# Head groups of 6, 7, 7, 6, 6, a second path for four token tiles, and another order of the first two units in a fused local-attention and gated-MLP kernel

## The chip, the core and the metric

The kernel runs on one core of a Trainium2 chip. The time of a run is in device microseconds (us), and lower is better. The engines are TensorE (PE, with its weight load PEld), VectorE (DVE), ScalarE (ACT), GpSimd (POOL) and SyncE (SP). DMA is issued from the queues of SP, ACT and POOL. Each engine runs its own instructions in the order in which they stand, and waits on semaphores for the others.

## What is computed

```python
xn = layernorm(x)                          # x: 2048 tokens of 640 features, f32
q, k, v = split(xn @ wqkv)                 # 32 heads of 20
# token t attends to t, t-2, ..., t-14 (window 8, dilation 2), masked below 0
s = softmax(q.k * 20**-0.5) @ v, then @ wo
g = silu(((xn @ w_gate) * (xn @ w_up)) @ w_down)   # hidden width 1536
out = x + s * g
```

All inputs are f32. Products are made at f32 accuracy by splitting each operand into a high part (fp32r) and a low part and adding three products: high by high, high by low, low by high.

## The kernel before

**Tokens.** Partition p holds 16 consecutive tokens, so a tile of 128 tokens takes one of the 16 from each partition. Tiles 0 to 7 are the even ones, 8 to 15 the odd ones, and so the neighbours at distance 2 stand in the same partition, in the next tile. Attention is then elementwise work on DVE over whole tiles. Only the first seven places come from the partition above, by a DMA that shifts k and v by one partition.

**Units and pieces.** A unit is one group of heads with one parity: `GROUPS` gives the heads of each of five groups, `UN` the ten units (u = 2 times group plus parity). `qkv(u, i)` makes q, k and v of one unit for one tile: 15 matmuls (three products by five feature blocks), with 3 x 20 x heads columns, into one of four `q` buffers of PSUM. ACT copies k and v into `kv` and q into one of two q tiles in SBUF. `attention(u)` is a generator of DVE work on the unit's tiles. `advance(budget)` draws some of its instructions into the program beside the matmuls, so that the order on DVE is written by these budgets. A piece is `gate_up(f, ch)`: 128 hidden columns by 512 tokens (four tiles), 15 matmuls for gate and 15 for up. `finish` multiplies the two: on DVE where an attention is running, else on ACT and POOL. Each unit after the second is followed by some pieces. Then follow the output projection and a down projection of 112 products.

**From x to the transposed operand.** Every matmul needs xn with features on partitions, split into high and low (`xT_tile`; four tiles share an `xc` buffer). There are two ways:

- Tiles 0 to 7: DVE takes the moments (`moments`), works out 1/std (`rstd`) and normalizes in place (`apply`). PE transposes five blocks of 128 columns into PSUM (`trans`, line 243), ACT copies the high part (line 244), DVE subtracts for the low part (line 245).
- Tiles 8 to 15: the moments are taken from the tile as it is first loaded. Then the tile is loaded again over itself from `xq` (`load_xq`), a copy in HBM in which the quarters of the tokens and of the features have changed places, so that VectorE's transposes within blocks of 32 finish the job (`trans_odd`). A row there holds quarters of four tokens, so the means and 1/std are spread to the right rows by small matmuls against a selection matrix (`spread`, line 263), and each tile is normalized in four pieces of 160 columns. ACT copies the high part, DVE subtracts the low part (line 275).

**The start.** PE first multiplies the identity with itself (`idle_product`) until operands are there. Weights are loaded raw (`wraw`, three buffers, in the order of the SP queue) and split: high part on ACT (line 85), low part on POOL (line 86), in later groups by a DMA that adds. Before, the program goes: tiles 0 and 1, their qkv of unit 0, half of the first piece, tiles 2 and 3, and so on, with tiles 8 to 15 prepared while PE does unit 0 and the pieces of the first two hidden blocks; then all eight tiles of unit 1; the attention of unit 0 is started during unit 1.

Of the kernel before, what the change touches and what calls it, by code (L numbers as in the profile page):

```python
# [13 lines left out]
AF = mybir.ActivationFunctionType  # L14
# [5 lines left out]
P = 128  # L20
S, D, F = 2048, 640, 1536
H, DH = 32, 20
W, DIL = 8, 2
# [27 lines left out]
def kernel(  # L51
# [114 lines left out]
    ident = st([P, P], "lg", 2)  # L166
    make_identity(nc, ident)

    def idle_product():

        nc.tensor.matmul(pt([P, 3, P], "q", 4), ident, ident.unsqueeze(1).to_broadcast([P, 3, P]), start=True,
                         stop=True)

    for _ in range(4):
        idle_product()
    eps_t = st([P, 1], "eps", 1)
    nc.vector.memset(eps_t, EPS)

# [15 lines left out]
    def moments(s0, n, mv=None):  # L194
        stats = st([P, n, 2, 6], "stats", 2)
        mv = st([P, n, 2], "mv", 2) if mv is None else mv
        for i in range(n):
            for a in range(2):
                nc.vector.bn_stats(stats[:, i, a, :], xt[s0 + i][:, a * HALF:(a + 1) * HALF])
            nc.vector.bn_aggr(mv[:, i, :], stats[:, i])  # L200
        return mv
# [20 lines left out]
    def apply(y, m, r):  # L222
        nc.vector.tensor_scalar(y, y, m, r, op0=ALU.subtract, op1=ALU.mult)
# [14 lines left out]
    def trans(s, later=False):  # L238
        hi, lo = xT_tile(s)
        for k0, k1 in ((0, 4), (4, KD)):  # L240
            p = pt([P, k1 - k0, P], "q", 4)
            for k in range(k0, k1):
                nc.tensor.transpose(p[:, k - k0, :], xt[s][:, k * P:(k + 1) * P], ident)  # L243
            nc.scalar.activation(hi[:, k0:k1, :], p, AF.Copy)
            halves.append(lambda p=p, k0=k0, k1=k1: nc.vector.tensor_sub(lo[:, k0:k1, :], p,  # L245
                                                                         hi[:, k0:k1, :].bitcast(F32)))
        if not later:
            low_parts()

    mvo = st([P, NE, 2], "mvo", 1)
    mro = st([P, 2, NE], "mro", 1)
    mrq = st([P, NQ, 2, NE], "mrq", 1)

    def load_xq(s, n, t):
        nc.sync.dma_start(t, xq[:, s - NE:s - NE + n, :])

    def spread():

        p = pt([P, NQ, 2, NE], "q", 4)
        for a in range(NQ):
            nc.tensor.matmul(p[:, a], sel[:, a], mro, start=True, stop=True)  # L263
        nc.scalar.activation(mrq, p, AF.Copy)

    def trans_odd(s):
        for a in range(NQ):
# [5 lines left out]
        nc.scalar.activation(hi, y, AF.Copy)  # L273
        low_parts()
        halves.append(lambda: nc.vector.tensor_sub(lo, y, hi.bitcast(F32)))
# [30 lines left out]
    def qkv(u, i, runs=ALL_RUNS, at=None, act=None):  # L306

        g, r = UN[u]
        c = GROUPS[g] * DH
        p = pt([P, 3 * c], "q", 4)  # L310
        t0 = (i % TPC) * P
        for n, (a, b, k) in enumerate(runs):
            if n == at:
                act()
            nc.tensor.matmul(p, xT[(r * NE + i) // TPC][a][:, k, t0:t0 + P], wq[g][b][:, k], start=n == 0,  # L315
                             stop=n == len(runs) - 1, skip_group_check=act is not None)
        nc.scalar.activation(kv_t[u][:, :, W - 1 + i, :], p[:, c:].rearrange("p (a c) -> p a c", a=2), AF.Copy)  # L317
        nc.scalar.activation(q_t[u][:, i, :], p[:, :c], AF.Copy)
# [91 lines left out]
    def gate_up_half(f, ch, n, p, c=slice(0, CH), **parts):  # L410
        mm3(p[:, c], [([t[:, k, n, :] for t in wf[f]], [t[:, k, c] for t in xT[ch]]) for k in range(KD)], **parts)
# [38 lines left out]
        while unfinished:  # L450
            unfinished.pop(0)()

    def gate_up_first(f, ch):

        pp = [pt([P, CH], "g", 2), pt([P, CH], "u", 2)]
        for parts, first in ((ALL3[:2], True), (ALL3[2:], False)):
            for n in range(2):
                gate_up_half(f, ch, n, pp[n], slice(0, CH // 2), parts=parts, first=first, last=not first)
        return pp


# [197 lines left out]
        return lambda: None  # L659


    norm(0, 1)
    mv1 = moments(1, 1)
    split_wq(0, nc.gpsimd, (0, 2))
# [2 lines left out]
    norm(1, 1, mv1)  # L667
    split_wq(0, nc.gpsimd, (3, KD))
    load_x(12, 1, xa[:, 0:1])
    begin_unit(0, False)  # L670
# [3 lines left out]
    qkv(0, 0, hh[:3] + lh[:3] + hh[3:] + lh[3:] + hl, 2 * KD + 3, lambda: trans(1))  # L674
    moments(3, 1, mv2[:, 1:2])
    load_x(13, 1, xa[:, 1:2])
    split_wf(0, nc.gpsimd, range(KD + 1))
    norm(2, 2, mv2)
    qkv(0, 1)
    split_wf(1, nc.gpsimd, range(KD + 1))  # L680
    zero_front(0)
    part0 = gate_up_first(0, 0)
    trans(2)
    trans(3)
    mask = st([1, NE, W], "mask", 1)
    nc.gpsimd.memset(mask, 0.0)
    for i in range(NE - 1):
        nc.gpsimd.memset(mask[:, i, :W - 1 - i], MASKED)
    sel = st([P, NQ, P], "ot", 2)
    nc.gpsimd.tensor_copy(sel.rearrange("p q (b i) -> p q b i", i=QB),  # L690
                          ident.rearrange("p (q i) -> p q i", i=QB).unsqueeze(2).to_broadcast([P, NQ, NQ, QB]))
# [8 lines left out]
    moments(10, 2, mvo[:, 2:4])  # L700
    load_xq(8, 4, xc[:, 4:8])
    trans(7)
    load_wf(2)
    qkv(0, 4)
    qkv(0, 5)
    moments(12, 2, mvo[:, 4:6])
    moments(14, 2, mvo[:, 6:8])
    load_xq(12, 3, xa)
    load_xq(15, 1, xd)
    nc.vector.tensor_copy(mro[:, 0, :], mvo[:, :, 0])  # L710
    rstd(mvo[:, :, 1], mro[:, 1, :], NE)
    gate_up(0, 1, amid=(spread,))
    trans_odd(8)
    trans_odd(9)
    qkv(0, 6)
    trans_odd(10)
    qkv(0, 7)
    trans_odd(11)
    gate_up(1, 1, amid=(lambda: trans_odd(12),))
    trans_odd(13)  # L720
    begin_unit(1)
    for i in range(8):
        if i == 3:
            running.append((0, attention(0)))
        if i == 2:
            load_wq(1, ((0, 3), (3, 5)))
            low_parts()
        if i < 2:
            trans_odd(14 + i)
        qkv(1, i)  # L730
        advance(PACE * 1.9)
    running.append((1, attention(1)))
    split_wq(1, nc.gpsimd)
    gate_up(0, 2)
    gate_up(1, 2)
    gate_up(0, 3)
    split_wf(2, nc.gpsimd)
    gate_up(1, 3)

    pieces = [(f, ch) for f in range(2, KF - 2) for ch in range(NCH)]  # L740
# [153 lines left out]
```

## Time and profile before

| | |
|---|---|
| time, median of 3 runs | 773.0 us (772.5 to 773.0) |
| time of the profiled execution | 772.99 us |
| its span, first to last instruction | 771.0 us |
| PE busy in the span | 763.1 us |
| DVE, ACT, POOL busy | 622.4, 251.2, 103.0 us |
| granted TensorE clock | 1.000 |

The profile page gives busy times, the chain of work that ended last, the costliest groups of instructions and the DMA issues. The span is 2.0 us shorter than the profiled execution's own time, and that time agrees with the median. A row of a timeline reads: start, length, engine, line, operation, what it writes and reads, count, and in brackets the idle time before it with what ended it. A row of the chain reads: start, length, engine, line. Lines are those of the kernel before; in the changed kernel the same code stands some lines lower.

### The profile page before, as it was taken

The page shows a single profiled execution, that of the slowest core. Times are in us where ns is not written, and L with a number is a line of the kernel's source. Part 1 is how long each engine was busy: PE and PEld are TensorE (multiplying, and loading weights), DVE is VectorE, ACT ScalarE, POOL GpSimd, SP SyncE. Part 2 cuts the span into 40 slices and gives each one's busy share as a digit, 9 for nine tenths or more (in the row PEclk, how much of TensorE's full clock was granted, in tenths as well). Part 3 has the DMA queues.
Part 4 walks back from the last instruction along what each step waited for, and adds up shares of the span by engine and source line. Part 5 has one row for each costly group of instructions (what it writes and reads, how often), then busy time and mean ns, then how long its engine had stood idle before and what let it go on. Part 6 is the DMA issues. An engine that isn't in the chain of part 4 may idle for free.

```text
span 771.0 us, 10626 instructions
## 1 busy us (share of the span) xinstructions
PE 763.1 (99%) x4214; PEld 703.7 (91%) x4214; DVE 622.4 (81%) x615; ACT 251.2 (33%) x519; POOL 103.0 (13%) x111
## 2 busy tenths in 40 slices
PE   8999999999999999999999999999999999999997
PEld 6889898898988989989899898888999999999997
DVE  6889899989959999599996999980377577777775
ACT  5333322132221241122411222213365564444442
POOL 5301110102001010000100000005387500000000
PEclk9999999999999999999999999999999999999999
DMA  9172441448043390423824213462887465555533
GB/s 323 73 235 83 90 119 55 87 148 144 28 112 75 100 203 29 115 62 113 176 55 115 63 57 101 107 179 66 201 248 217 168 250 175 193 185 185 184 103 137
DMA packets 82277, 103.33 MB, mean 134 GB/s; under 512 B 19036, under 2 KB 61376, under 8 KB 82100
## 3 DMA queue, kind: packets, MB, share of 16 engines
q1 hardware_dynamic: 72400, 82.85, 34.4%
q0 software_dynamic: 4128, 10.70, 8.1%
q10 hardware_dynamic: 5700, 9.11, 4.3%
q8 instruction: 33, 0.54, 0.3%
q14 instruction: 16, 0.13, 0.0%
HBM read 65.23 MB, written 28.31 MB: 121 GB/s over the span
## 4 chain that ended last, share of the span: by engine, by line
PE 97%; DMA 2%; ACT 0%; POOL 0%; DVE 0%; issue 0%; SPq 0%; POOLq 0%
PE q L315 26%; PE u L101 21%; PE g L101 21%; PE q L632 11%; PE q L101 9%; PE u L632 5%; PE g L632 3%; DMA wraw<-in_wgu 1%; DMA wraw<-in_wqkv 1%; PE q L243 0%; POOL wql L86 0%; ACT wf L85 0%; SPq L148 0%; PE q L263 0%; DVE xc L245 0%
## 5 line engine op out<-in xcount | busy, mean ns | idle before, releaser
L101 PE MATMUL u<-xc,wf 128*128 128x512 f32 (+1 forms) x735 | 171.8, 385 | 0.0
L101 PE MATMUL g<-xc,wf 128*128 128x512 f32 (+1 forms) x735 | 171.7, 385 | 0.0
L101 PEld LDWEIGHTS u<-xc,wf 128*128 128x128 f32 x735 | 136.0, 188 | 27.4
L101 PEld LDWEIGHTS g<-xc,wf 128*128 128x128 f32 x735 | 135.9, 188 | 26.6
L315 PE MATMUL q<-wqh,xc 128*128 128x420 f32 (+2 forms) x800 | 153.0, 334 | 2.0 <-DVE xc L245 1.2
L315 PEld LDWEIGHTS q<-wqh,xc 128*128 128x128 f32 x800 | 138.9, 188 | 3.8 <-DVE xc L245 1.4
L351 DVE TENSOR_TENSOR t<-q,kv 128x2240 f32<-128x2240 f32 (+2 forms) x40 | 90.6, 2286 | 28.8 <-DMA kv<-kv 28.6
L376 DVE TENSOR_TENSOR t<-lg,kv 128x2240 f32<-128x2240 f32 (+2 forms) x40 | 90.8, 2289 | 0.9
L355 DVE TENSOR_REDUCE lg<-t 128x112 f32<-128x2240 f32 (+2 forms) x40 | 90.5, 2281 | 0.0
L423 ACT ACTIVATE gs<-g 128x512 f32<-128x512 f32 x48 | 28.6, 596 | 174.0 <-PE g L101 164.9
L315 PE MATMUL q<-wql,xc 128*128 128x420 f32 (+2 forms) x400 | 81.8, 334 | 0.0
L317 ACT ACTIVATE kv<-q 128x280 f32<-128x280 f32 (+2 forms) x80 | 30.7, 383 | 139.4 <-PE q L315 137.4
L315 PEld LDWEIGHTS q<-wql,xc 128*128 128x128 f32 x400 | 69.9, 188 | 0.0
L384 DVE TENSOR_TENSOR t<-t,t 128x2240 f32<-128x2240 f32 (+2 forms) x30 | 68.7, 2289 | 0.8
L632 PE MATMUL q<-xc,wf 128*128 128x320 f32 x432 | 67.2, 309 | 0.0
L632 PEld LDWEIGHTS q<-xc,wf 128*128 128x128 f32 x432 | 64.3, 188 | 0.0
L92 POOL DMA_DIRECT2D wf<-in_wgu x10 | 8.7, 873 | 277.7 <-ACT wf L91 224.4
L101 PE MATMUL q<-wf,wf 128*128 128x320 f32 x156 | 35.5, 309 | 0.0
L92 POOL DMA_DIRECT2D wql<-in_wqkv x8 | 10.2, 1281 | 133.1 <-ACT wql L91 132.5
L101 PEld LDWEIGHTS q<-wf,wf 128*128 128x128 f32 x156 | 26.1, 188 | 0.0
L434 DVE TENSOR_TENSOR hs<-u,gs 128x512 f32<-128x512 f32 x38 | 25.9, 683 | 0.0
L86 DVE TENSOR_TENSOR wf<-ot,wf 128x640 fp32r<-128x640 f32 x13 | 14.2, 1091 | 12.8 <-ACT wf L85 12.8
(167 smaller groups left out, 919.4 us busy)
## 6 DMA issues: line engine op xcount, KB each, us to landing
h_scr<-hs SPq DMA_DIRECT2D x48, 256.0 KB, 2.2
wraw<-in_wgu SPq DMA_DIRECT2D x12, 640.0 KB, 6.6
wf<-in_wgu POOLq DMA_DIRECT2D x10, 640.0 KB, 6.3
t<-h_scr SPq DMA_DIRECT2D x8, 768.0 KB, 7.7
hs<-s_scr SPq DMA_DIRECT2D x16, 320.0 KB, 4.5
gs<-in_x SPq DMA_DIRECT2D x16, 320.0 KB, 4.9
wraw<-h_scr SPq DMA_DIRECT2D x12, 384.0 KB, 6.0
out<-q SPq DMA_DIRECT2D x14, 320.0 KB, 3.8
```

Of the source, the lines that this page charges most:

```text
L86: eng.tensor_sub(lo, raw, hi.bitcast(F32))
L92: nc.gpsimd.dma_start(lo, src, accum_op=ALU.add)
L101: nc.tensor.matmul(acc, a, b, start=first and n == 0, stop=last and n == len(runs) - 1)
L315: nc.tensor.matmul(p, xT[(r * NE + i) // TPC][a][:, k, t0:t0 + P], wq[g][b][:, k], start=n == 0, stop=n == len(runs) - 1, skip_group_check ...
L317: nc.scalar.activation(kv_t[u][:, :, W - 1 + i, :], p[:, c:].rearrange("p (a c) -> p a c", a=2), AF.Copy)
L351: nc.vector.tensor_mul(prods[j], q.rearrange("p i c -> p (i c)").unsqueeze(1).to_broadcast([P, 2, NE * c]), places(0, j))
L355: nc.vector.tensor_reduce(out=lg[:, :, j:j + 2].rearrange("p n a -> p a n"), in_=heads(prods.pop(j)), op=ALU.add, axis=AX.X)
L376: nc.vector.tensor_mul(heads(t), pw, heads(places(1, j)))
L384: nc.vector.tensor_add(acc, acc, t)
L423: nc.scalar.activation(gs, pp[0], AF.Copy)
L434: nc.vector.tensor_mul(hs, pp[1], gs)
L632: nc.tensor.matmul(p, y[:, i, k], wd_t[name][k][:, l], start=new and r == 0, stop=r == len(runs) - 1, skip_group_check=True)
```

## The change

1. `GROUPS` goes from 5, 6, 7, 7, 7 to 6, 7, 7, 6, 6 heads.
2. Tiles 4 to 7 take the second way too: loaded again from `xq` (which now holds tiles 4 to 15), normalized in quarters, transposed by VectorE. `spread` becomes one matmul for four tiles instead of four matmuls for eight: VectorE first puts each mean and 1/std into its own quarter (`mrb`).
3. Tiles 4 to 15 are done in three batches of four: moments, second load, `spread`, `trans_quarters`. Units 0 and 1 and the first two hidden blocks are interleaved in the same batches. The attention of unit 0 is started after the last batch.
4. The first eight pieces and unit 1 are followed by 2 pieces ahead of unit 2, and units 2, 3, 4 by 3, 3, 4 pieces (before: none, then 4 after each).
5. At the start: tiles 2 and 3 are normalized one at a time; tile 2 is transposed between the two halves of `gate_up_first` and tile 3 inside `qkv(0, 2)`; the zeros of kv, the mask and the selection matrix are made on POOL first of all; the last idle product has 256 columns instead of 384.

PE in the start, before (`q` is PSUM, `xc` the transposed operand, `t_67` tiles 2 and 3, `wf` gate and up weights, `lg_89` the identity):

```order
L101 MATMUL u_267<-xc_140,wf_209 128x256 x10
L101 MATMUL g_266<-xc_140,wf_210 128x256 x5
L101 MATMUL u_267<-xc_140,wf_210 128x256 x5
L243 MATMUL q_298<-lg_89,t_67 128x128 x4
L243 MATMUL q_304<-lg_89,t_67 128x128
L243 MATMUL q_309<-lg_89,t_67 128x128 x4
L243 MATMUL q_315<-lg_89,t_67 128x128
L315 MATMUL q_358<-wqh_134,xc_140 128x300 x5
L315 MATMUL q_358<-wql_135,xc_140 128x300 x5
```

The same place now:

```order
L102 MATMUL u_290<-xc_162,wf_238 128x256 x10
L244 MATMUL q_311<-lg_89,t_67 128x128 x4
L244 MATMUL q_317<-lg_89,t_67 128x128
L102 MATMUL g_289<-xc_162,wf_239 128x256 x5
L102 MATMUL u_290<-xc_162,wf_239 128x256 x5
L327 MATMUL q_332<-wqh_156,xc_162 128x360 x5
L244 MATMUL q_338<-lg_89,t_67 128x128 x4
L244 MATMUL q_344<-lg_89,t_67 128x128
L327 MATMUL q_332<-wql_157,xc_162 128x360 x5
```

Tile 2's transposes stand ten matmuls earlier, tile 3's five matmuls later than the first matmul of `qkv(0, 2)`.

DVE after the moments of tiles 4 to 7, before (`xc_81` holds these tiles as loaded):

```order
L219 TENSOR_SCALAR rstd_346<-rstd_346 128x4
L220 TENSOR_TENSOR r_345<-rstd_346 128x4
L223 TENSOR_SCALAR xc_81<-xc_81,mv_332,r_345 128x640 x4
L245 TENSOR_TENSOR xc_430<-q_431,xc_430 128x4x128
L245 TENSOR_TENSOR xc_430<-q_437,xc_430 128x128
L245 TENSOR_TENSOR xc_430<-q_442,xc_430 128x4x128
L245 TENSOR_TENSOR xc_430<-q_448,xc_430 128x128
```

and now:

```order
L221 TENSOR_TENSOR mro_108<-rstd_375 128x4
L264 TENSOR_TENSOR mrb_109<-mro_108,t_67 128x32
L224 TENSOR_SCALAR xc_81<-xc_81,mrq_110 128x160 x4
L282 STREAM_TRANSPOSE ot_446<-xc_81 128x640
L224 TENSOR_SCALAR xc_81<-xc_81,mrq_110 128x160 x4
L282 STREAM_TRANSPOSE ot_454<-xc_81 128x640
L287 TENSOR_TENSOR xc_448<-ot_446,xc_448 128x5x128
L224 TENSOR_SCALAR xc_81<-xc_81,mrq_110 128x160 x4
L282 STREAM_TRANSPOSE ot_500<-xc_81 128x640
L287 TENSOR_TENSOR xc_448<-ot_454,xc_448 128x5x128
```

Between the moments and the first normalizing instruction there are now the multiplication into quarters (L264), a matmul and a second load of 1280 KB (on their own engines); the transposes have gone from PE to DVE, and the low parts come between the tiles.

PE from the first full piece's up product to unit 0's second four tiles, before:

```order
L101 MATMUL u_461<-xc_140,wf_253 128x512 x10
L101 MATMUL u_461<-xc_140,wf_254 128x512 x5
L243 MATMUL q_517<-lg_89,xc_81 128x128 x4
L243 MATMUL q_523<-lg_89,xc_81 128x128
L315 MATMUL q_530<-wqh_134,xc_430 128x300 x5
L315 MATMUL q_530<-wql_135,xc_430 128x300 x5
L315 MATMUL q_530<-wqh_134,xc_430 128x300 x5
L315 MATMUL q_550<-wqh_134,xc_430 128x300 x5
L315 MATMUL q_550<-wql_135,xc_430 128x300 x5
L315 MATMUL q_550<-wqh_134,xc_430 128x300 x5
L101 MATMUL g_593<-xc_430,wf_209 128x512 x10
L101 MATMUL g_593<-xc_430,wf_210 128x512 x5
```

and now, from the spread on:

```order
L274 MATMUL q_439<-mrb_109,t_67 128x32
L102 MATMUL g_458<-xc_162,wf_277 128x512 x10
L102 MATMUL g_458<-xc_162,wf_278 128x512 x5
L102 MATMUL u_459<-xc_162,wf_277 128x512 x10
L102 MATMUL u_459<-xc_162,wf_278 128x512 x5
L327 MATMUL q_513<-wqh_156,xc_448 128x360 x5
L327 MATMUL q_513<-wql_157,xc_448 128x360 x5
L327 MATMUL q_513<-wqh_156,xc_448 128x360 x5
L327 MATMUL q_533<-wqh_156,xc_448 128x360 x5
L327 MATMUL q_533<-wql_157,xc_448 128x360 x5
L327 MATMUL q_533<-wqh_156,xc_448 128x360 x5
```

The transposes of tiles 6 and 7 are gone, and only one piece stands between the spread of the means and the four tiles' qkv, which now follow each other.

```diff
-GROUPS = [5, 6, 7, 7, 7]
+GROUPS = [6, 7, 7, 6, 6]
+FIRST = 4
...
-    for _ in range(4):
-        idle_product()
+    for n in (3, 3, 3, 2):
+        idle_product(n)
...
+    def moments_of_four(s):
+        a, b = s - FIRST, (s - FIRST) // 4
+        moments(s, 4, mvo[:, a:a + 4])
+        nc.vector.tensor_copy(mro[:, b, 0], mvo[:, a:a + 4, 0])
+        rstd(mvo[:, a:a + 4, 1], mro[:, b, 1], 4)
+        nc.vector.tensor_mul(mrb[:, b], mro[:, b].unsqueeze(1).to_broadcast([P, NQ, 2, 4]),
+                             blk.unsqueeze(2).unsqueeze(3).to_broadcast([P, NQ, 2, 4]))
...
+    def spread(s):
+
+        b = (s - FIRST) // 4
+        p = pt([P, NQ, 2, 4], "q", 4)
+        nc.tensor.matmul(p, sel, mrb[:, b], start=True, stop=True)
+        nc.scalar.activation(mrq[:, :, b], p, AF.Copy)
+
+    def trans_quarters(s):
+        b, i = divmod(s - FIRST, 4)
         for a in range(NQ):
-            apply(xt[s][:, a * QC:(a + 1) * QC], mrq[:, a, 0, s - NE:s - NE + 1], mrq[:, a, 1, s - NE:s - NE + 1])
+            apply(xt[s][:, a * QC:(a + 1) * QC], mrq[:, a, b, 0, i:i + 1], mrq[:, a, b, 1, i:i + 1])
...
+    begin_unit(0)
+    mask = st([1, NE, W], "mask", 1)
...
-    part0 = gate_up_first(0, 0)
-    trans(2)
-    trans(3)
...
-    norm(4, 4)
-    qkv(0, 2)
+    part0 = gate_up_first(0, 0, lambda: trans(2))
+    qkv(0, 2, at=KD, act=lambda: trans(3))
+    moments_of_four(4)
+    load_xq(4, 4, xc[:, 0:4])
     qkv(0, 3)
     gate_up(0, 0, part=part0)
-    trans(4)
-    trans(5)
-    moments(8, 2, mvo[:, 0:2])
-    gate_up(1, 0, amid=(lambda: trans(6),))
...
+    spread(4)
+    trans_quarters(4)
+    trans_quarters(5)
+    gate_up(1, 0)
+    trans_quarters(6)
+    trans_quarters(7)
+    low_parts()
+    for i in range(4, 8):
+        qkv(0, i)
+    load_wf(2)
+    moments_of_four(8)
     load_xq(8, 4, xc[:, 4:8])
...
+    gate_up(0, 1, amid=(lambda: spread(8),))
+    for i in range(8, 12):
+        trans_quarters(i)
+    low_parts()
+    moments_of_four(12)
...
+    gate_up(1, 1)
     begin_unit(1)
...
+    for i in range(4):
+        qkv(1, i)
+    gate_up(0, 2, amid=(lambda: spread(12),))
+    for i in range(12, 16):
+        trans_quarters(i)
+    low_parts()
+    running.append((0, attention(0)))
+    gate_up(1, 2)
+    for i in range(4, 8):
+        if i == 6:
+            gate_up(0, 3)
             load_wq(1, ((0, 3), (3, 5)))
-            low_parts()
...
+            split_wf(2, nc.gpsimd)
         qkv(1, i)
         advance(PACE * 1.9)
     running.append((1, attention(1)))
     split_wq(1, nc.gpsimd)
...
     gate_up(1, 3)
...
-    for u in range(2, len(UN)):
-        unit(u)
-        for _ in range(4 if u + 1 < len(UN) else len(pieces)):
+    COUNT = (0, 2, 3, 3, 4, 4, 4, 4, 4)
+    for u in range(1, len(UN)):
+        if u > 1:
+            unit(u)
+        for _ in range(COUNT[u] if u + 1 < len(UN) else len(pieces)):
```

More of the change, by code (lines that the diff above doesn't have):

```diff
@@ L167, with idle_product @@
     make_identity(nc, ident)
-    def idle_product():
-        nc.tensor.matmul(pt([P, 3, P], "q", 4), ident, ident.unsqueeze(1).to_broadcast([P, 3, P]), start=True,
+    def idle_product(n):
+        nc.tensor.matmul(pt([P, n, P], "q", 4), ident, ident.unsqueeze(1).to_broadcast([P, n, P]), start=True,
                          stop=True)
-    for _ in range(4):
-        idle_product()
+    for n in (3, 3, 3, 2):
+        idle_product(n)
     eps_t = st([P, 1], "eps", 1)
@@ L248, in trans @@
             low_parts()
-    mvo = st([P, NE, 2], "mvo", 1)
-    mro = st([P, 2, NE], "mro", 1)
-    mrq = st([P, NQ, 2, NE], "mrq", 1)
-    def load_xq(s, n, t):
-        nc.sync.dma_start(t, xq[:, s - NE:s - NE + n, :])
-    def spread():
-        p = pt([P, NQ, 2, NE], "q", 4)
-        for a in range(NQ):
[L263 to L267, printed above, removed]
-            apply(xt[s][:, a * QC:(a + 1) * QC], mrq[:, a, 0, s - NE:s - NE + 1], mrq[:, a, 1, s - NE:s - NE + 1])
+    NS = NT - FIRST
+    mvo = st([P, NS, 2], "mvo", 1)
+    mro = st([P, NS // 4, 2, 4], "mro", 1)
+    mrb = st([P, NS // 4, NQ, 2, 4], "mrb", 1)
+    mrq = st([P, NQ, NS // 4, 2, 4], "mrq", 1)
+    def moments_of_four(s):
[5 more added lines that the diff above has]
+                             blk.unsqueeze(2).unsqueeze(3).to_broadcast([P, NQ, 2, 4]))
+    def load_xq(s, n, t):
+        nc.sync.dma_start(t, xq[:, s - FIRST:s - FIRST + n, :])
+    def spread(s):
[5 more added lines that the diff above has]
+        b, i = divmod(s - FIRST, 4)
+        for a in range(NQ):
+            apply(xt[s][:, a * QC:(a + 1) * QC], mrq[:, a, b, 0, i:i + 1], mrq[:, a, b, 1, i:i + 1])
         y = st([P, KD, P], "ot", 2)
@@ L458, in gate_up_first @@
                 gate_up_half(f, ch, n, pp[n], slice(0, CH // 2), parts=parts, first=first, last=not first)
+            if first:
+                amid()
         return pp
@@ L659, in gather @@
         return lambda: None
+    begin_unit(0)
+    mask = st([1, NE, W], "mask", 1)
+    nc.gpsimd.memset(mask, 0.0)
+    for i in range(NE - 1):
+        nc.gpsimd.memset(mask[:, i, :W - 1 - i], MASKED)
+    sel, blk = xe[:, 2, :P], xe[:, 2, P:P + NQ]
+    nc.gpsimd.memset(blk, 0.0)
+    for a in range(NQ):
+        c = slice(a * QB, (a + 1) * QB)
+        nc.gpsimd.memset(blk[c, a:a + 1], 1.0)
+        nc.gpsimd.tensor_copy(sel[c].rearrange("p (q i) -> p q i", i=QB),
+                              ident[c, c].unsqueeze(1).to_broadcast([QB, NQ, QB]))
     norm(0, 1)
@@ L708 @@
+    load_wf(2)
+    moments_of_four(8)
+    load_xq(8, 4, xc[:, 4:8])
+    gate_up(0, 1, amid=(lambda: spread(8),))
[3 more added lines that the diff above has]
+    moments_of_four(12)
     load_xq(12, 3, xa)
     load_xq(15, 1, xd)
[L710 to L719, printed above, removed]
@@ L733 @@
     split_wq(1, nc.gpsimd)
[L734 to L737, printed above, removed]
     gate_up(1, 3)
@@ L872 @@
     arrays["xb"] = lay(arrays["x"].reshape(S, NQ, KD, QB).transpose(0, 2, 1, 3).reshape(S, D))
-    odd = arrays["x"].reshape(NQ, QB, NE, DIL, NQ, QC)[:, :, :, 1]
-    arrays["xq"] = lay(odd.transpose(3, 1, 2, 0, 4).reshape(P, NE, D))
+    tiles = arrays["x"].reshape(NQ, QB, NE, DIL, NQ, QC).transpose(4, 1, 3, 2, 0, 5).reshape(P, NT, D)
+    arrays["xq"] = lay(tiles[:, FIRST:])
     q3 = np.asarray(A_wqkv).reshape(D, 3, D)
```

30 lines of the change are left out of this document (4 added, 26 removed).

## The prediction

> **What bounds the kernel now.** I read the page's busy times first, then the chain that ended last, PE's waits and the windows.
>
> ```profile
> span 771.0 us, 10626 instructions
> PE 763.1 (99%) x4214; PEld 703.7 (91%) x4214; DVE 622.4 (81%) x615; ACT 251.2 (33%) x519; POOL 103.0 (13%) x111
> PE q L171 <- POOL lg masks.py:199: 1.4, 1, 1.4
> PE q L315 <- DVE xc L245: 1.2, 1, 1.2
> PE q L315 <- ACT xc L244: 0.9, 2, 0.6
> POOL wql L86 <- ACT wqh L85: 5.4, 1, 5.4
> 700.00:771.00 71.00, 66.59 (x455) 66.33 (x453) 51.31 (x69) 28.04 (x48) 0.00 (x0) 1.00 0.48 165
> ```
>
> PE is busy for 763.1 of 771.0 us. Its idle time is 1.4 + 1.2 + 0.9 at the start (the rows of waits give total, times, longest) and 4.4 in the last 71 us (66.59 busy), behind its last matmul. Between 20 us and the tail it never waits. So only two things move the end: the matmul time itself, and waits that are made or taken away. The chain shows the start and the pieces that the change touches (start, length, what):
>
> ```profile
> 9.31 7.81 DMA wraw<-in_wgu
> 17.14 1.65 ACT wf L85 x5
> 18.79 0.49 ACT xc L244
> 19.30 0.70 DVE xc L245
> 20.05 4.40 PE q L315 x30
> 24.44 1.79 PE g L101 x15
> 28.04 1.09 PE q L243 x10
> 32.55 0.55 PE q L243 x5
> 36.55 0.55 PE q L243 x5
> 44.68 0.80 PE q L263 x8
> 59.96 16.40 PE q L315 x120
> 76.36 3.40 PE g L101 x15
> 103.56 19.20 PE q L315 x120
> 196.36 22.40 PE q L315 x120
> ```
>
> The second gate/up block (issued 9.31, landed 17.12) is split on ACT ahead of the copies of tile 2; PE stands still until 20.05, and from there it is full.
>
> **PE's own work.** The unit rows (120 matmuls) give 16.40, 19.20 and 22.40 us for 5, 6 and 7 heads. Two units per group: before 2 x (16.40 + 19.20 + 3 x 22.40) = 205.6, after 2 x (3 x 19.20 + 2 x 22.40) = 204.8: **-0.8**. The transposes of tiles 4 to 7 go: 1.09 + 0.55 + 0.55 = **-2.2**. The spread took 0.80 for four matmuls; three remain at about 0.2 (twice the columns, so 0.2 to 0.4): **-0.2**, or +0.4 at worst. PE sum: -3.2. DVE, ACT and DMA rows that replace these lie beside PE unless they come late, which is the rest of this text.
>
> **The start.** Two of the sixteen tile products of unit 0 and 1 get wider ahead of the wait at 20.05: 2 x (19.20 - 16.40) / 8 = 0.7 us, which falls into that wait. So behind the wait PE loses not 0.8 but 1.5 us: **-0.7** more. Tile 3's transposes move from ahead of the wait to behind it: **+0.55**. The wait itself: PE used to need the low part on DVE, because its PSUM buffer was that of tile 2's first transposes. Now tile 3 comes later, the buffers turn differently, and PE needs only the first copy of ACT: -0.7 (the DVE row). Against that the weights grow.
>
> ```profile
> wraw<-in_wqkv SPq DMA_DIRECT2D x5, 150.0 KB, 4.0
> 7.00:11.00 4.00, 3.30 (x22) 2.52 (x20) 3.08 (x11) 2.06 (x7) 3.90 (x5) 1.00 0.98 346
> 11.00:15.00 4.00, 3.73 (x28) 3.51 (x27) 3.38 (x14) 3.43 (x12) 2.40 (x5) 1.00 1.03 403
> ```
>
> Five loads of 150 KB become 180: 0.154 MB more ahead of the awaited block, at 346 to 403 GB/s (last column) 0.4 us, since DMA is full (share 0.98 and 1.03). The block's issue also waits for POOL's splits, a fifth longer, but the queue is not empty by then. I take 17.12 + 0.45, PE full again at 17.57 + 1.65 + 0.02 + 0.49 + 0.07 = 19.8: **-0.25** (bounds -0.7 with no delay, +0.4 if issue sets it). The POOL work moved ahead of the first split lies in the 5.4 us that POOL waits before it (the last of the rows of waits), and the shorter idle product gains nothing behind that wait. Start: -0.7 + 0.55 - 0.25 = -0.4.
>
> **The new chain of tiles 4 to 7.** This is where a wait can arise. From 19.8 PE does a tile's qkv (2.4), tile 3's transposes (0.55), another qkv (2.4), half a piece (3.6), the spread (0.2), a piece (6.8): `qkv(0, 4)` starts at 35.8. Each tile's product needs the high part at once and the low part after ten of 15 matmuls, so tile 6's low part is wanted at 35.8 + 4.8 + 1.6 = 42.2. DVE's side:
>
> ```profile
> 20.90 0.88 DVE L199 BATCH_NORM_STATS2 stats<-xc 128x6 f32<-128x320 f32 x2
> 23.92 0.83 DVE L199 BATCH_NORM_STATS2 stats<-xc 128x6 f32<-128x320 f32 x2
> 26.24 0.16 DVE L220 TENSOR_TENSOR r<-rstd 128x4 f32<-128x4 f32 x1
> xc<-in_xq SPq DMA_DIRECT2D x1, 1280.0 KB, 6.7
> wraw<-in_wgu SPq DMA_DIRECT2D x1, 640.0 KB, 4.0
> 45.88 1.18 DVE L223 TENSOR_SCALAR xc<-xc,mrq 128x160 f32<-128x160 f32 x4 [1.89 <-DMA xc<-in_xq]
> 49.80 1.29 POOL L437 TENSOR_TENSOR hs<-hs,gs 128x512 f32<-128x512 f32 x1 [11.24 <-ACT hs L436]
> 50.33 1.45 DVE L275 TENSOR_TENSOR xc<-ot,xc 128x640 fp32r<-128x640 f32 x1 [0.33 <-ACT xc L273]
> 56.35 0.78 DVE L275 TENSOR_TENSOR xc<-ot,xc 128x640 fp32r<-128x640 f32 x1
> ```
>
> Tile 3's low part ends about 22.5 (19.8 + 0.8 of PE + 0.55 + 0.5 on ACT + 0.9 on DVE). The moments of four tiles take about 4.0 (20.90 to 23.92 plus one tile), so the second load is issued at 26.5: SP waits there, and behind it stand only writes of h and loads for later. The same 1280 KB took 6.7 us beside other loads; 640 KB alone took 4.0 (an answer for 109 to 118 us). Alone, 1280 KB should take 4.0 plus 655 KB at 403 GB/s = 5.6, an estimate from these rows. So it lands at 32.1 to 33.2. From the first normalizing piece to the third tile's low part the same code took 56.35 + 0.78 - 45.88 = 11.2 us, with 0.67 in it from one subtraction that took 1.45 instead of 0.78 while POOL multiplied. Tile 6 is ready at 43.3 to 44.4: 1.1 to 2.2 late; with the POOL product elsewhere and a load that lands by 31.4 it is in time. Bounds 0 and 2.2, and I take **+1.2** (near the lower row, since little else is loaded then). The Trainium skill (SBUF — State Buffer, Who interferes with whom) says that a VectorE instruction with two SBUF inputs and a GpSimd instruction that reads SBUF block each other; the 1.45 beside 0.78 agrees, and by that rule the product of the new piece near 36 us costs the same 0.67, which the 11.2 holds already.
>
> The spread itself waits on DVE's means: moments at 26.5 plus 1.6 for 1/std and the quarters (24.9 to 26.4 on DVE before, and one small multiplication), so 28.1 against PE's 28.8: no wait, 0.3 at worst. Only this spread has half a piece ahead of it; for the next batch the two sides meet almost evenly: DVE needs 0.8 + 4.0 + 1.7 = 6.5 behind tile 6's low part, PE has 0.8 + 2.4 + 3.4 = 6.6 to do. **+0.1** (0 to 0.5). Later batches: the load of tiles 8 to 11 is issued about 48 and has until 55, that of 12 to 15 about 69 with two pieces ahead: no wait at 5.6 to 6.7, with 1 to 3 us to spare.
>
> **Attention starts later.**
>
> ```profile
> 69.51 3.56 DVE L351 TENSOR_TENSOR t<-q,kv 128x1600 f32<-128x1600 f32 x2
> 138.55 4.22 DVE L351 TENSOR_TENSOR t<-q,kv 128x1920 f32<-128x1920 f32 x2
> 177.47 1.16 DVE L387 TENSOR_TENSOR q<-t 128x960 f32<-128x960 f32 x1
> 105.45 0.36 SPq L392 DMA_DIRECT2D o_scr<-q  x1
> 109.05 0.27 ACT L318 ACTIVATE q<-q 128x120 f32<-128x120 f32 x1 [2.69 <-DMA o_scr<-q]
> ```
>
> Unit 0's attention began at 69.51. Now it stands behind the low part of tile 15: that batch's load lands about 75, and four tiles take 12.2 (the 11.2 above and one more subtraction), so about 87. Six heads took 138.55 to 178.6, 40.1 us with the products and the wait in it: it ends about 127, and the q tile is free 3.6 later (105.45 to 109.05), at 130.7. Unit 2 fills that q tile. From 35.8 PE does twelve tiles (28.8), eight pieces (54.4), two spreads (0.4) and the waits (1.3), and reaches unit 2 at 120.7; four PSUM buffers let it run 4 x 2.8 = 11.2 further, to 131.9. Reserve 1.2, against 4.1 before (103.56 + 9.6 - 109.05): **0**, but this cover is thin. Units 2 and 3 have 22.4 + 3 x 6.8 = 42.8 us on PE and seven heads on DVE, at most 46.8 (40.1 x 7/6), so DVE loses at most 4.0 in each: unit 3's q tile is free at 127 + 40.1 + 3.6 = 170.7 and wanted at 120.7 + 42.8 + 11.2 = 174.7, unit 4's at 217.5 at worst and wanted at 217.5, and from there four pieces give 5 back per unit. The last units have six heads instead of seven, so the tail gains no wait.
>
> **Sum.** PE -3.2, start -0.4, tiles 4 to 7 +1.2, second spread +0.1: -2.3. Span 771.0 - 2.3 = 768.7; with the 2.0 us around it (772.99 - 771.0; the profiled execution equals the median) **770.7 us**.
>
> **Rivals.**
>
> 1. *No wait at all.*
>
> ```profile
> 22.00:24.00 2.00, 2.00 (x16) 2.00 (x15) 1.93 (x8) 0.00 (x0) 1.26 (x10) 1.00 0.15 54
> ```
>
> The load lands by 31.4 and POOL's product misses DVE: -2.3 - 1.3 = -3.6, **769.4**. For it: DMA is nearly empty then (share 0.15 from 22 to 24 us). Against: 640 KB alone took 4.0, and twice that in 4.9 would need 655 KB in 0.9. The Trainium skill (DMA: Bandwidth & Descriptors, Anatomy of one DMA) gives a load from GpSimd's queue as 2.0 us plus bytes over 436 GB/s; by that, as an estimate, 1.31 MB takes 5.0 and lands at 31.5, which is this rival. The trace differs from it on 640 KB, 4.0 against 3.5. Chance 0.15.
>
> 2. *The thin reserves break.* The third load lands 3 us later than I have it, or DVE loses as much among POOL's products: attention begins at 90, unit 2's q tile is free at 133.7, and PE waits 1.8 at its fifth tile. 770.7 + 1.8 = **772.5**, no change that can be told. For it: the reserve falls from 4.1 to 1.2, and every DVE delay of three batches adds up in it. Against: the third batch has two pieces between spread and use. Chance 0.14.
>
> 3. *Slow second loads.* One mechanism, three places: each batch's qkv waits for a load that DVE cannot ask for before the moments are done.
>
> ```profile
> t<-in_xq SPq DMA_DIRECT2D x1, 960.0 KB, 10.2
> ```
>
> The neighbouring load of the same kind took 10.2. With that for all three, the first batch is 26.5 + 10.2 + 11.2 - 42.2 = 5.7 late; the second is 2.9 late at tile 10 and the third 4.3 at tile 15 (same steps, with PE having 23 us between a batch's third tile and the next one's): 770.7 - 1.3 + 12.9 = **782**. It decides from 8.0 us on, where the first wait alone eats the 3.6. Against: that load was queued behind 1280 KB and 640 KB, and now each batch loads alone. Chance 0.08.
>
> 4. *DVE becomes the bound.* Four tiles add about 4 x 1.2 us to its 622.4; it has 149 us idle, much of it behind the attention. That gives no time of its own but through rival 2.
>
> **Chances and range.** Forecast 0.60 (its own range 769.6 to 771.7), rivals 0.15, 0.14 and 0.08, the rest 0.03. What a measurement of this kernel can tell from no change is about 0.2%, 1.55 us: faster is below 771.4, slower above 774.5. Faster: rival 1 and nearly all of the forecast, 0.70; same: rival 2 and the forecast's end, 0.18; slower: rival 3 and the rest, 0.12. The range runs from just below rival 1 to just above rival 2, 769.2 to 773.2; rival 3 is left out.
>
> **What would show it.** PE's start in the changed profile: full from about 19.8, the wait there ended by ACT and not DVE. The critical rows of PE transposes after 28 us gone. A PE wait of about 1 us at tile 6 of unit 0, ended by the DVE subtraction, near 42 us; the landing of the second load 5.6 to 6.7 after issue. No PE wait on ACT at unit 2's fifth tile near 131. I am wrong if PE shows a wait over 2.2 us at 36 to 46, waits in the second or third batch, or if PE becomes full later than 20.5.

## The result: slower by 1.4 per cent, with no more idle time on PE

The changed kernel takes 783.4 us (median of 4 runs, 783.3 to 784.1) against 772.9 (772.5 to 773.0) for the kernel before in the same session: a ratio of 1.0136 (95% interval 1.0124 to 1.0149). The forecast was 770.7 with a range of 769.2 to 773.2. It has the wrong sign.

The page of the changed kernel:

```profile
span 781.3 us, 10618 instructions
PE 773.9 (99%) x4192; PEld 704.9 (90%) x4192; DVE 631.2 (81%) x638; ACT 251.6 (32%) x520; POOL 106.8 (14%) x120
PEclk9999999999999999999999999999999999999999
```

PE has 22 matmuls fewer than before and is busy 10.8 us longer, 773.9 against 763.1, at an unchanged granted clock (1.00 in the windows below). The idle time of PE did not grow: 781.3 - 773.9 = 7.4 us against 771.0 - 763.1 = 7.9. Its waits (total, times, longest):

```profile
PE q L172 <- POOL lg masks.py:199: 1.4, 1, 1.4
PE q L327 <- ACT xc L245: 0.6, 1, 0.6
PE q L274 <- DVE mrb L264: 0.3, 1, 0.3
PE q L244 <- issue: 0.3, 1, 0.3
PE q L244 <- PE q L172: 0.3, 1, 0.3
```

So none of the waits of the prediction is the answer. The chain of the changed kernel (start, length, what) shows what is:

```profile
18.76 1.08 PE q L327 x5
35.17 10.20 PE q L327 x60
60.12 9.99 PE q L327 x60
122.29 22.67 PE q L327 x120
144.95 3.49 PE g L102 x15
310.93 19.98 PE q L327 x120
558.85 70.40 PE q L102 x480
645.09 5.27 PE q L646 x36
```

A unit of six heads takes 19.98 us instead of 19.20, one of seven 22.67 instead of 22.40, and 15 matmuls of gate or up 3.50 or 3.49 instead of 3.40. The matmuls are the same in count, shape and type. The 480 matmuls of the output projection (70.40; 70.39 before) and the 36 of a down product (5.27; 5.28) have kept their pace. By matmul:

| columns | before, ns | changed, ns | more, ns |
|---|---|---|---|
| 512 (gate, up) | 226.7 | 233.3 | 6.6 |
| 420 (7 heads) | 186.7 | 188.9 | 2.2 |
| 360 (6 heads) | 160.0 | 166.5 | 6.5 |
| 320 (output and down projection) | 146.6 | 146.7 | 0 |

The windows of both kernels, cut at unit 2 and at the output projection (stretch, length, PE busy, clock, DMA share, GB/s; the changed kernel first, then the kernel before):

```profile
0.00:122.30 122.30, 119.25 (x605) 1.00 0.51 159
122.30:558.85 436.55, 436.55 (x2102) 1.00 0.38 99
558.85:781.30 222.45, 218.14 (x1488) 1.00 0.59 189
```

```profile
103.56:548.36 444.80, 444.80 (x2162) 1.00 0.41 102
548.36:771.00 222.64, 218.23 (x1488) 1.00 0.58 189
```

In the middle stretch the profile shows PE busy throughout in both kernels. At the old pace the changed one would need there four units of seven and four of six heads, 4 x 22.40 + 4 x 19.20 = 166.4, and 76 blocks of 15, 258.4, together 424.8. It needs 436.5. That stretch alone holds 11.7 of the 12.6 us by which the span misses the forecast.

### The profile page after: what moved, and what is told of

It reads as the page before. It is cut to its first block, busy times and chain, and to the rows that moved or that the text cites. A ratio compares the mean times of both kernels' runs of the same rounds, so it can differ in the third digit from the quotient of the medians.

```text
span 781.3 us, 10618 instructions
## 1 busy us (share of the span) xinstructions
PE 773.9 (99%) x4192; PEld 704.9 (90%) x4192; DVE 631.2 (81%) x638; ACT 251.6 (32%) x520; POOL 106.8 (14%) x120
## 4 chain that ended last, share of the span: by engine, by line
PE 97%; DVE 1%; ACT 1%; DMA 0%; SPq 0%; issue 0%; ACTq 0%
PE q L327 27%; PE u L102 21%; PE g L102 21%; PE q L646 11%; PE q L102 9%; PE u L646 5%; PE g L646 3%; DMA wraw<-in_wqkv 0%; ACT xc L245 0%; ACT wf L86 0%; ACTq L334 0%; SPq L149 0%; PE q L244 0%; DVE t L224 0%; DVE xc L246 0%
## 5 line engine op out<-in xcount | busy, mean ns | idle before, releaser
L102 PE MATMUL u<-xc,wf 128*128 128x512 f32 (+1 forms) x735 | 176.3, 391 | 0.0
L102 PE MATMUL g<-xc,wf 128*128 128x512 f32 (+1 forms) x735 | 176.0, 391 | 0.0
L327 PE MATMUL q<-wqh,xc 128*128 128x360 f32 (+1 forms) x800 | 156.3, 338 | 0.8 <-ACT xc L245 0.6
L388 DVE TENSOR_TENSOR t<-lg,kv 128x1920 f32<-128x1920 f32 (+1 forms) x40 | 90.8, 2288 | 0.8
L363 DVE TENSOR_TENSOR t<-q,kv 128x1920 f32<-128x1920 f32 (+1 forms) x40 | 90.9, 2287 | 0.5
L367 DVE TENSOR_REDUCE lg<-t 128x96 f32<-128x1920 f32 (+1 forms) x40 | 90.4, 2280 | 0.0
L327 PE MATMUL q<-wql,xc 128*128 128x360 f32 (+1 forms) x400 | 83.6, 339 | 0.0
L329 ACT ACTIVATE kv<-q 128x240 f32<-128x240 f32 (+1 forms) x80 | 30.9, 386 | 155.3 <-PE q L327 153.1
L396 DVE TENSOR_TENSOR t<-t,t 128x1920 f32<-128x1920 f32 (+1 forms) x30 | 68.7, 2289 | 0.7
L381 DVE TENSOR_REDUCE sm<-lg 128x48 f32<-128x384 f32 (+1 forms) x10 | 5.8, 579 | 26.1 <-ACT lg L379 26.1
```

What stands on the lines that cost most here:

```text
L102: nc.tensor.matmul(acc, a, b, start=first and n == 0, stop=last and n == len(runs) - 1)
L363: nc.vector.tensor_mul(prods[j], q.rearrange("p i c -> p (i c)").unsqueeze(1).to_broadcast([P, 2, NE * c]), places(0, j))
L367: nc.vector.tensor_reduce(out=lg[:, :, j:j + 2].rearrange("p n a -> p a n"), in_=heads(prods.pop(j)), op=ALU.add, axis=AX.X)
L381: nc.vector.tensor_reduce(out=sm[:, 0, :], in_=e, op=ALU.add, axis=AX.X)
L388: nc.vector.tensor_mul(heads(t), pw, heads(places(1, j)))
L396: nc.vector.tensor_add(acc, acc, t)
```

## Where a tile lies

The order of the work does not change a matmul, but the change also added and enlarged small tiles: `mvo` and `mro` go from 64 to 96 bytes per partition, `mrq` from 256 to 384, and `mrb` is new with 384. Together that is 576 bytes. SBUF tiles lie behind each other in the order of their first allocation, so all that follows moves: in the program as built, `kv0` begins at byte 125248 of a partition instead of 124672, `wqh` at 169280 instead of 159232, `wf` at 187200 instead of 186368. (`wqh` moves further because the mask and the two q tiles are now allocated ahead of it.) All of these were multiples of 256 and are now 64 past one. `xc`, the transposed operand, lies ahead of the small tiles and stays at 35584, a multiple of 256. In gate and up `xc` is the moving operand and `wf` the stationary one; in qkv `xc` is stationary and `wqh` and `wql` move. In both, the two operands have lost 64 bytes against each other. "On the grid" means below: at a multiple of 256 bytes.

## The experiments

The small tiles are followed by a padding tile, `gap`, of 24 floats. In both kernels its size moves everything behind it and nothing else. The theories of the first four runs: **A**, the places of the tiles slowed the matmuls; **B**, the new order did, through what now runs beside them.

**Changed kernel, tiles back on the grid** (64 bytes less of padding):

```diff
-    st([P, 24], "gap", 1)
+    st([P, 8], "gap", 1)
```

> The changed kernel, with one padding tile in SBUF of 8 floats per partition instead of 24. Nothing else moves in the program: all tiles behind the small norm tiles (kv, q, wqh, wql, wf and so on) start 64 bytes lower and so again at multiples of 256 bytes, as in the kernel before; the changed kernel has them 64 bytes past one. Theory A (addresses: the added norm tiles, 576 bytes, moved the weights and k/v against xc, and each matmul of qkv and gate/up pays for it, 512 columns 3.50 instead of 3.40 us per 15, 6 heads 19.98 instead of 19.20 per unit, 7 heads 22.67 instead of 22.40): the old paces return; 1410 full gate/up matmuls x 6.6 ns + 720 x 6.5 + 480 x 2.3 = 15.1 us less, 768.3, up to 770 if PE then waits more. Theory B (the new order, the head groups or the transposes on VectorE slow the matmuls, by traffic of other engines): 783.4 stays.

Measured: 769.9 us (5 runs, 769.8 to 770.1) against 773.0 for the kernel before in the same session, ratio 0.9957 (0.9941 to 0.9973). Its page, its windows in the same cuts, and rows of its chain:

```profile
span 768.2 us, 10618 instructions
PE 760.7 (99%) x4192; PEld 700.6 (91%) x4192; DVE 632.6 (82%) x638; ACT 251.8 (33%) x520; POOL 105.1 (14%) x120
```

```profile
0.00:120.05 120.05, 117.36 (x605) 1.00 0.52 162
120.05:545.10 425.05, 425.05 (x2104) 1.00 0.40 101
545.10:768.20 223.10, 218.25 (x1487) 1.00 0.59 188
```

```profile
18.77 1.04 PE q L327 x5
35.13 10.13 PE q L327 x60
59.78 9.60 PE q L327 x60
120.05 22.40 PE q L327 x120
142.45 3.40 PE g L102 x15
304.85 19.20 PE q L327 x120
```

The old paces are back, and the middle stretch takes 425.05, the 424.8 of above. A is confirmed and B falls: the instructions and their order are the same as in the slow kernel. This is also the fastest version of the study: the change as it was meant gains 3.1 us, and its span, 768.2, is near the forecast's 768.7. `wf` lies at 187136 here, 768 bytes above its place in the kernel before, while `xc` has not moved. That is three times 256 and no multiple of 512, so a shift by an odd multiple of 256 did no harm.

**Kernel before, 64 bytes off:**

```diff
-    st([P, 24], "gap", 1)
+    st([P, 40], "gap", 1)
```

> The kernel before, with the same padding tile at 40 floats instead of 24: kv, q, wqh, wql, wf and what lies behind start 64 bytes past a multiple of 256, as in the changed kernel; the program is that of before. Theory A: 1410 x 6.6 ns + 240 (6 heads) x 6.5 + 720 (7 heads) x 2.3 = 12.6 us more, and up to 1.6 for the 240 matmuls of 5 heads: 785 to 787. Theory B: 773.

Measured: 785.2 us (4 runs, 784.7 to 785.5), ratio 1.0159 (1.0144 to 1.0174), span 783.0. Units take 16.57, 19.98 and 22.67, gate and up 3.50: the paces of the changed kernel, in the old program. A padding of 64 bytes that nobody reads costs 12 us.

**Kernel before, 128 and 32 bytes off** (`gap` of 56 and of 32 floats):

> The kernel before with the padding tile at 56 floats: the same tiles start 128 bytes past a multiple of 256. Theory A with a period of 64 or 128 bytes cannot be told from 773 here (a period of 64 is excluded if the 64-byte shift costs); with a period of 256 bytes or more the 512-column pace is above 3.40 us per 15 again. Theory B: 773.

> The kernel before with the padding tile at 32 floats: the same tiles start 32 bytes past a multiple of 256. Theory A: slower than 773 as with 64 bytes, if what counts is any start off the 128 or 256 byte grid: 785 to 787; 773 if only the 64-byte place is bad. Theory B: 773.

Measured, one run each: 787.6 (span 785.6; units 16.67, 19.68 to 20.00 and 23.18 to 23.19, gate and up 3.48 to 3.50) and 785.5 (span 783.5; 16.60, 19.99, 22.70 to 22.80 and 3.50). A shift of 32 or of 128 bytes costs no less than one of 64. The 320 columns kept their pace (5.27 and 5.29 a down product, 70.39 the output projection in both).

**Which operand.** The next four move one group of tiles by 64 bytes in the kernel before (16 floats of padding ahead of it, 48 behind it), or all tiles together. The theories: **M**, the place of the moving operand counts; **S**, that of the stationary one; **R**, the places of both against each other.

```diff
+    st([P, 16], "padA", 1)
     split_wf(0, nc.gpsimd, range(KD + 1))
+    st([P, 48], "padB", 1)
```

> The kernel before with only the four wf tiles 64 bytes off the 256-byte grid (64 bytes of padding ahead of them, 192 behind); xc, wqh, wql, kv, gs and hs stay on it. wf is the stationary operand of gate and up, xc the moving one; in qkv xc is stationary and wqh/wql move. Theory M (the place of the moving operand sets the pace): no change, 15 gate or up matmuls in 3.40 us and units at 16.40, 19.20 and 22.40, span 771. Theory S (the stationary operand) and theory R (both have to lie alike): gate and up at 3.50, units unchanged, 1440 matmuls by 6.6 ns = +9.5, span 780.5.

The same pads around the first `split_wq(0, ...)`:

> The kernel before with only wqh and wql 64 bytes off the grid. Theories M and R: units at 16.57, 19.98 and 22.67, that is 2 x (0.17 + 0.78 + 3 x 0.27) = +3.5, gate and up unchanged at 3.40, span 774.5. Theory S: no change, span 771.

The same pads around `xc = st(...)`:

> The kernel before with only the four xc tiles (x transposed, high and low parts) 64 bytes off the grid. Theory M: gate and up at 3.50, units unchanged, span 780.5. Theory S: units slow (16.57, 19.98, 22.67), gate and up at 3.40, span 774.5. Theory R: both slow, span 783-784.

All tiles, by the padding ahead of the first large one:

```diff
-    st([P, 32], "skip", 1)
+    st([P, 48], "skip", 1)
```

> The kernel before with every tile, from the first on, moved by the same 64 bytes. Theory R (only the place of the two operands against each other counts): no change, span 771. Theories M and S (an absolute grid of 256 bytes): all slow as with 64 bytes in the gap, span 783 or above, gate and up at 3.50.

Measured, one run each, beside 773.0 for the kernel before:

| moved by 64 bytes | time, us | span | 15 of gate, up | 5, 6, 7 heads |
|---|---|---|---|---|
| nothing | 773.0 | 771.0 | 3.40 | 16.40, 19.20, 22.40 |
| wf | 786.5 | 784.5 | 3.50 | 16.79, 19.74, 22.93 |
| wqh, wql | 777.3 | 775.3 | 3.40 | 16.57, 19.99, 22.68 |
| xc | 781.9 | 780.0 | 3.43 | 16.40, 20.00, 23.19 |
| all tiles | 774.0 | 772.0 | 3.40 | 16.40, 19.20, 22.40 |

The last row settles one thing: it is not an absolute grid. With all operands 64 bytes off, but alike, the paces are the old ones (the 0.9 us arises ahead of unit 2, which begins at 104.42 instead of 103.56). M and S fall too, since a shift of `xc` alone, and of either partner alone, costs time. R is nearest, but two rows are not its own. The shift of `xc` slows gate and up only to 3.43, where one of `wf` gives 3.50; the two shift the operands against each other in opposite directions, but that the direction is the reason is not shown. And with `wf` moved, qkv slowed by 0.4 to 0.5 us a unit although its own operands lie exactly where they lay. Two ways remained: some of the tiles behind `wf`, which the pads move by 256 bytes, or something that the gate and up matmuls leave behind for the next.

**Control for the first way:** only the tiles behind `wf` move by 256 bytes.

```diff
     split_wf(0, nc.gpsimd, range(KD + 1))
+    st([P, 64], "padB", 1)
```

> A control for the run that moved wf alone: there mask, ot, gs, hs and the tiles behind them moved by 256 bytes too, and qkv became slow although its own operands had not moved. Here only these later tiles move by 256 bytes, wf stays. If the place of wf slowed the qkv units behind it: no change, span 771, units at 16.40, 19.20, 22.40, gate and up at 3.40. If the later tiles did it: units at 16.79, 19.74 and 22.93, span 774.

Measured: 774.0 us (773.4 for the kernel before beside it), span 771.9, units 16.40, 19.20, 22.40, gate and up 3.40. These tiles are not the cause. The 0.9 of the span is again the start.

**Test of the second way:** every tile on the grid, and one small matmul in the middle of each unit from unit 2 on.

```diff
+        if u > 1 and i == 4:
+            nc.tensor.matmul(pt([P, 32], "q", 4), xT[r * NE // TPC][0][:, 0, :P], wq[g][0][:, 0, :32], start=True, stop=True)
```

> The kernel before with one small matmul (32 columns, result unread) put ahead of the fifth tile of each of the eight units from unit 2 on; all tiles stay on the grid. Theory H (a run of matmuls keeps the rhythm into which what came before has put it): the 60 matmuls behind the small one leave 160.0 ns and 186.7 ns, to 164-167 and 189-193, until the next block: 60 x 4.7 ns = 0.28 us or more per unit, span 771 + 8 x (0.1 + 0.3) = 774.2. Theory N (the places of the operands alone set the pace): the small matmul only, span 771.0 + 8 x 0.1 = 771.8, and 160.0 and 186.7 on both sides of it.

Measured: 777.3 us, span 775.3. The chain of this run at a unit of six heads and one of seven:

```profile
102.99 9.60 PE q L317 x60
112.59 0.02 PE q L313
112.60 9.97 PE q L317 x60
122.57 3.45 PE g L101 x15
196.65 11.20 PE q L317 x60
207.87 11.70 PE q L317 x60
```

Sixty matmuls of six heads take 9.60 ahead of the small one and 9.97 behind it, of which about 0.1 is its own; without it the unit takes 2 x 9.60. The distances from start to start, read from the trace, show a steady rhythm on both sides:

```
ahead of it:  160 160 160 160 160 160 160 160 160 160 160 160 ...
behind it:    254 166 163 165 165 164 164 166 163 164 166 163 165 165 164 164 ...
```

It lasts until the unit's end, 59 matmuls later, without recovering. The first gate block behind the unit shows 233 231 233 236 224 231 236 228 233 231 226 and then is back at 226.7. The eight small matmuls make 2 x 0.37 and 6 x 0.50 in the units and 8 x 0.05 in the gate blocks behind them, 4.1 of the 4.3 us by which the span is longer (774.2 was expected for the span; the units of seven heads lose more than was allowed for). Elsewhere two differences of this one run nearly cancel: unit 2 begins 0.6 earlier, and the output projection takes 0.65 longer. The small matmul also takes one of the four PSUM buffers and so turns their order for all that follows; since the first sixty matmuls of the next units are back at 9.60 and 11.20, that is not the cause. With `wf` moved, the units ran at 164.5 ns in the same rhythm (164 166 163 165 165 164). So theory H holds for the small matmul: the pace of a run of matmuls depends on the rhythm in which it starts, and a run can stay in a slower one. That the same is what slowed qkv when only `wf` moved rests on the likeness of the rhythm.

**The parts of the change.** The new groups alone in the kernel before, and the old groups in the realigned changed kernel:

```diff
-GROUPS = [5, 6, 7, 7, 7]
+GROUPS = [6, 7, 7, 6, 6]
```

> The kernel before with the new groups of 6, 7, 7, 6, 6 heads alone; no tile moves. By the prediction's steps: units -0.8, wider tiles inside the first wait -0.7, the wait itself +0.4 by the larger weights: span 769.9 (769.5 to 770.2), units at 19.20 and 22.40. If the groups themselves slowed the matmuls, units at 19.98 and 22.67 and span 773 or above.

> The realigned changed kernel with the old groups of 5, 6, 7, 7, 7 heads. By the same steps backwards: units +0.8, wider tiles +0.7, the wait -0.4, so 1.1 above the realigned changed kernel's span of 768.2: 769.3 (769.0 to 769.6). If the interplay of the groups with the new order matters (unit 2's tile fills in time only with the new groups, or the opposite), a PE wait appears or goes and the span leaves that range.

Measured for the first: 774.0, span 771.9, 2.0 more than expected; units at 19.20 and 22.40. From unit 2 on it is the sum by steps: unit 2 begins at 110.83 against 103.56, and the rest of the span is 661.1 against 667.4, 6.3 less, where the unit rows say 6.4 less (two units of 22.40 for 19.20, four the other way round). The miss is in the start: PE had a wait of 1.7 us at the first transposes, and the clock granted behind it was half (the column behind the count):

```profile
PE q L243 <- issue: 1.7, 1, 1.7
8.00:10.00 2.00, 1.42 (x8) 0.71 0.95 338
10.00:12.00 2.00, 2.00 (x8) 0.50 0.98 389
```

No other run of the study shows this, and it was one run; whether the groups have to do with it is open.

Measured for the second: 774.5, span 772.7, where 769.3 was expected. The cause is new waits:

```profile
PE q L274 <- DVE mrb L264: 1.9, 2, 1.6
PE q L327 <- ACT xc L245: 1.7, 3, 0.9
PE q L327 <- DVE xc L287: 0.9, 2, 0.6
PE u L102 <- DVE hs L446: 0.4, 1, 0.4
```

PE's waits rise by 3.3 us against the realigned kernel with the new groups. In the first batches PE's work per tile is what covers DVE's chain, and with five heads a tile gives 0.35 us less of it. So the parts don't add up: in this run the new order needs the new groups.

## Why the prediction was wrong, step by step

**The step that failed is "PE's own work".** It priced each matmul by the rows of the kernel before ("The unit rows give 16.40, 19.20 and 22.40") and counted only how many there are of which width. The count was right. The price was not a constant of the shape: 19.98, 22.67 and 3.50 were measured in the changed kernel, and realigning it, with no other edit, took 13.5 us off its time. The opening claim, "only two things move the end: the matmul time itself, and waits", stood; I then looked at waits for the rest of the text. The diff shows the new tiles, and the code the paddings between tiles (`skip`, `gap`, `gap0`) and the rounding of the weight rows to 64 floats; a look at what the added 576 bytes do to the tiles behind would have raised the question. It could not have priced it, since no row of the kernel before shows a tile off the grid. No rival had this mechanism, so the chance of slower, 0.12, came for other reasons. None of the signs of being wrong that the prediction lists is the pace of a matmul either; of them the changed kernel shows only a wait of 0.3 in the second batch, which lies within the bounds given for it.

The realigned run tests the other steps, apart from this one:

- **Groups, -0.8:** right. The unit rows are again 19.20 and 22.40, and the run with the groups alone gives the sum from unit 2 on. The -0.7 for the wider tiles inside the first wait is separated by no run.
- **The start:** the wait ended by ACT and not by DVE, as forecast, but at 18.76 and 18.77 instead of 19.8, so the added weights did not delay the awaited block by the 0.45 that I took: it was issued at 9.26 and landed at most 6.9 us later, against 9.31 and 7.81 before. `qkv(0, 4)` starts at 35.13 (forecast 35.8), 0.7 better.
- **Tiles 4 to 7, +1.2:** the place was right, the size was not: 0.5. The second load was issued at 25.61 and landed in time for the first normalizing piece at 31.15; the estimate of 5.6 us holds. Rows of the realigned kernel's timeline, DVE, POOL and PE apart:

```profile
31.15 1.18 DVE L224 TENSOR_SCALAR xc<-xc,mrq 128x160 f32<-128x160 f32 x4 [3.63 <-DMA xc<-in_xq]
37.76 1.19 DVE L287 TENSOR_TENSOR xc<-ot,xc 128x640 fp32r<-128x640 f32 x1
40.85 1.71 DVE L287 TENSOR_TENSOR xc<-ot,xc 128x640 fp32r<-128x640 f32 x2
36.98 1.29 POOL L449 TENSOR_TENSOR hs<-hs,gs 128x512 f32<-128x512 f32 x1 [6.90 <-ACT hs L448]
36.57 1.76 PE L327 MATMUL q<-wqh,xc 128*128 128x360 f32 x10
39.01 1.92 PE L327 MATMUL q<-wqh,xc 128*128 128x360 f32 x10
```

The POOL product did meet a subtraction, for 1.19 - 0.78 = 0.4 us, where the prediction had 0.67. No list of waits shows a stop of PE here, but the distances between starts do: 200 and 270 ns at tile 5's eleventh matmul, which is the first to read its low part (0.15 us lost), 266 and 268 at tile 6's (0.2 us), and from the first of these on the run has left 160.0 for the slow rhythm of about 164.7, for another 0.15. Together that is the 10.13 of the row at 35.13 against 9.60. Theory H is at work in the changed kernel itself.
- **Second spread, +0.1 (0 to 0.5):** 0.4. What is late is not the moments but 1/std: ACT has to issue the shifting DMAs of kv first (`ACTq L334`, to 47.35), and only then takes the square root. The realigned kernel's chain there:

```profile
46.44 0.91 ACTq L334
47.39 0.31 ACT rstd L206
48.73 0.20 DVE mrb L264
49.07 0.38 PE q L274 x2
```

- **Third batch and the q tile of unit 2:** no wait, as forecast; unit 2 runs its 120 matmuls from 120.05 in 22.40, and rival 2 did not happen. Rival 3 did not either: the second loads took a median of 6.1 us.
- **The tail, "gains no wait":** off by 0.6 in this execution. The output projection waits for its second tile, whose attention result is loaded from HBM, transposed and split. From the realigned kernel's waits and timeline:

```profile
PE q L102 <- ACT wf L86: 0.6, 1, 0.6
541.62 1.84 SPq L500 DMA_DIRECT2D o<-o_scr  x4
548.14 0.84 DVE L507 STREAM_TRANSPOSE ot<-o 128x640 f32<-128x640 f32 x1 [7.34 <-DMA o<-o_scr]
```

  The attention is not what is late: its last instruction on DVE ends at 510.5, against 516.9 in the kernel before. The load is issued 3.5 us earlier than before and PE arrives 3.3 earlier, but from the first issue to the transpose it takes 6.5 us, where the kernel before takes 5.0 (545.13 to 550.10) and the changed kernel and the run with the old groups 5.1. The run with the small matmuls, in the old order, has a like wait of 0.4. So this is one slow load; whether the change has to do with it is open.

From 768.7: -0.7 at the start, -0.7 at tiles 4 to 7, +0.3 at the second spread, +0.6 at the tail make 768.2, which is what was measured. That it came so near the forecast is partly luck, since errors of -1.4 and +0.9 offset each other. The split between the steps is also only good to about half a microsecond. The prediction's timeline reaches unit 2 at 120.7, but its sum puts it at 103.56 + 5.6 (two units of six heads for five) + 13.6 (two more pieces) - 1.5 (the terms that fall ahead of unit 2) = 121.3; measured was 120.05. The forecast was for a kernel whose tiles lie as they did before.

Of rival 1 the loads decide. The Trainium skill (DMA: Bandwidth & Descriptors, Anatomy of one DMA) gives 2.0 us plus bytes over 436 GB/s for a load from GpSimd's queue; by that, as an estimate, these 1.31 MB take 5.0 us. The trace, on SP's queue, has 31.15 - 25.61 = 5.5 from issue to first use. The estimate from the rows of the kernel before, 5.6, was closer.

## What to carry to other kernels

The price of a matmul that is taken from a profile holds, as these runs show, for the places at which its operands lay. Where a change adds or resizes a tile, compare where the large tiles lie before and after, and pad the small ones so that these keep their places against each other; here the changed kernel needed 64 bytes less of padding to turn a loss of 10.5 us into a gain of 3.1. And where PE is busy longer with fewer matmuls at the same clock, compare the mean distance of like matmuls before looking for a wait.

## What the runs showed of the hardware that was not expected

- The pace of fp32r matmuls that follow each other depends on the places of the two SBUF operands against each other. A shift of one of them by 32, 64 or 128 bytes cost up to about 6.6 ns of 226.7 with 512 columns and up to 6.7 of 160.0 with 360, and 2.2 to 6.6 of 186.7 with 420; a shift of both by the same 64 cost nothing, and 256 cost nothing. With 320 columns no shift cost anything in the mean, 146.6 ns. The down products kept it with `wf` shifted against `xc`. In the output projection the operands moved together in most runs; where `wf` alone or `wqh` and `wql` alone moved, its 480 matmuls took 70.40 us all the same.
- A run of such matmuls keeps its rhythm. One small matmul, or a stop of 0.15 us, changes 160.0 to about 164.5 ns for the rest of the unit, at the same places. With the tiles on the grid, gate and up found their way back within a dozen matmuls, the 360 and 420 columns did not before the next block.
- What in the reading of SBUF makes this rhythm, why 320 columns are spared, and why a shift of `xc` costs gate and up less than one of `wf`, none of these runs shows. The other distances below 256 bytes were not tried.
